# A third halving on VectorE in a single-query attention kernel, with shorter TensorE sums, another cut of the first K load and a whole last copy

## Chip, cores, metric

One core of a Trainium2 chip (trn2). The metric is the device time of one execution in microseconds (us); the median of several is given. The *span* in a profile is about 1.7 us shorter than the time. Only one core runs, so there is no second die to compare with. In the views PE is TensorE (matmuls), PEld its weight loads, DVE VectorE, ACT ScalarE, POOL GpSimd, and SPq the queue that issues loads. The granted TensorE clock is given where it matters.

## The reference

For 256 heads, one query of 128 numbers is compared with 4096 keys, and the softmax of the scores weighs 4096 values:

```python
B, H, Sq, Skv, Dh = 8, 32, 1, 4096, 128            # all bf16
scores = jnp.einsum('bhqd,bhkd->bhqk', q, k) * Dh ** -0.5
attn = softmax(scores, axis=-1)
out = jnp.einsum('bhqk,bhkd->bhqd', attn, v)
```

Each key and value is used once. K and V are 537 MB; all else is small.

## The kernel before

The work goes in 32 tiles of 8 heads. A tile of K, and one of V, is 128 partitions x 256 positions x 128 numbers, 8.39 MB. There are two K buffers and one V buffer; the last V takes a K buffer. The scores of a tile come in four chunks of 64 positions. VectorE multiplies K by q and adds the upper half of D to the lower. TensorE adds up the remaining 64 numbers, as eight slices of 8, through matmuls with the identity; 8 numbers are left. VectorE adds up these eight. In the views `kt` and `vt` are tiles of K and V, `ps` these sums, `sc` the scores, `av` the weighted values; `comb` is the copy of `av`, `op` the matmuls that gather it, and `stage` the finished rows.

```python
cuts = {                                   # pieces of a load; [C] where nothing is said
    ("k", 0): [C // 4, C // 4, C // 2],
    ("k", NT - 4): [C // 2] * 2,           # NT - 3, NT - 2 likewise
    ("k", NT - 1): [C // 4, C // 4, C // 2],
    ("v", NT - 1): [C // 2, C // 4, C // 8, C // 16, C // 32, LAST, LAST],
}
# ... load(): q is queued right behind the first piece of the first K

def product(t, lo, hi):
    for c0 in range(lo, hi, MC):           # MC = 64 positions
        part = kt[:, c0 : c0 + MC, :]
        nc.vector.tensor_tensor(out=part, in0=part, in1=qb..., op=ALU.mult)
        nc.vector.tensor_tensor(out=part[:, :, 0 : D // 2], in0=part[:, :, 0 : D // 2],
                                in1=part[:, :, D // 2 : D], op=ALU.add)

def sum_over_d(t, u):
    n = D // 2 // DS                       # DS = 8, so 8 matmuls
    for s in range(n):
        nc.tensor.matmul(ps[:], lhsT=ident[:],
            rhs=kt[:, u * UC : (u + 1) * UC, s * DS : (s + 1) * DS],
            start=(s == 0), stop=(s == n - 1))

# values_of(t): 64 matmuls "av", dealt to four column groups of the array
group = [0 if t == NT - 1 and C // 2 <= c0 < 3 * C // 4 else c0 // CB % TG ...]

def copy_of(t):
    n = CB if t < NT - 1 else CB // 2      # the last copy: half on ScalarE, half on VectorE
    nc.scalar.activation(out=comb[:, 0:n, :], in_=av[:, 0:n, :], func=ACT.Copy)
    if n < CB:
        nc.vector.tensor_copy(out=comb[:, n:CB, :], in_=av[:, n:CB, :])

# order in a tile t: issue K of t+1 and V of t; chunks 0 and 1; the av matmuls of
# tile t-1, which free V's buffer; chunks 2 and 3; softmax weights
```

## Time and profile before

| | before |
|---|---|
| median (3 runs, 1254.5 to 1254.62) | 1254.57 us |
| span of the profiled run | 1252.8 us |
| loaded | 537 MB, 429 GB/s over the span |
| busy: TensorE, VectorE, ScalarE | 554.0, 967.6, 343.3 us |
| mean granted TensorE clock | 0.685 |

In the groups of instructions of the page, the columns are: line, engine, operation, output and inputs, shapes and count | busy us, mean ns | idle us of the engine before them and what ended most of it. Two of VectorE's groups are compared later:

```profile
L175 DVE TENSOR_TENSOR kt<-kt,qb 128x8192 bf16<-128x8192 bf16 x128 | 565.2, 4415 | 181.9 <-DMA kt<-in_k_dram 175.3
...
L202 DVE TENSOR_REDUCE sc<-ps 128x64 f32<-128x512 f32 x128 | 87.8, 686 | 68.1 <-PE ps L190 68.1
```

The next view cuts the tail into stretches. In each line, after the stretch and its length, come the busy us of PE, PEld, DVE, ACT and POOL with their instruction counts, then the granted clock, the mean busy share of the 16 transfer engines and the GB/s.

```profile
1244.00:1246.00 2.00, 2.00 (x11) 0.87 (x10) 0.00 (x0) 0.00 (x0) 0.00 (x0) 1.00 0.62 247
1246.00:1247.00 1.00, 1.00 (x13) 0.47 (x11) 0.00 (x0) 0.00 (x0) 0.00 (x0) 1.00 0.44 156
1247.00:1248.00 1.00, 0.95 (x11) 0.33 (x7) 0.00 (x0) 0.00 (x0) 0.00 (x0) 1.00 0.07 26
```

Some engines are done by 1244, and one, roughly (0.07 of 16), still works after 1247. A load counts as landed only when all 16 are done.

### The profile page before, as it was taken

The numbers are of one execution on the slowest core, as the hardware profiler recorded it, in microseconds if no ns is written. First come the engines' busy times: TensorE is split into PE (matmuls) and PEld (weight loads), VectorE is DVE, ScalarE is ACT, GpSimd is POOL, SyncE is SP. The second block draws the span as 40 slices with busy tenths as digits, with TensorE's granted clock in tenths as the row PEclk, the third lists the DMA queues.
The fourth block names the chain that finished last, engine by engine and source line by source line (L and its number), as shares of the span: only waits on it lengthen the run. The fifth ranks groups of instructions, "written<-read, shape, count | busy, mean of one in ns | idle before, by whom it ended". The sixth has DMA issues, their size and how long they took to land.

```text
span 1252.8 us, 8134 instructions
## 1 busy us (share of the span) xinstructions
PE 554.0 (44%) x3299; PEld 202.6 (16%) x3299; DVE 967.6 (77%) x531; ACT 343.3 (27%) x625; POOL 6.0 (0%) x26
## 2 busy tenths in 40 slices
PE   2444543345534355333453334542445434545356
PEld 0111111111111111111111111111112111211112
DVE  7877887777977779777797777886778877977981
ACT  0333123331233321333213333123330333311333
POOL 1000000000000000000000000000000000000000
PEclk8667666667657767576765776666676766676777
DMA  9999999999999999999999999999999999999997
GB/s 404 435 436 432 434 435 433 434 432 434 435 434 436 434 429 429 431 432 433 434 434 436 430 436 436 436 434 435 432 427 427 437 433 432 434 420 431 430 439 311
DMA packets 11734, 537.53 MB, mean 429 GB/s; under 512 B 1840, under 2 KB 2096, under 8 KB 2352
## 3 DMA queue, kind: packets, MB, share of 16 engines
q1 hardware_dynamic: 11360, 536.94, 99.3%
q8 instruction: 26, 0.43, 0.1%
q10 hardware_dynamic: 336, 0.07, 0.0%
q14 instruction: 12, 0.10, 0.0%
HBM read 536.94 MB, written 0.07 MB: 429 GB/s over the span
## 4 chain that ended last, share of the span: by engine, by line
DMA 79%; PE 14%; DVE 6%; issue 0%; SPq 0%; another core or an unknown queue 0%; ACT 0%
DMA vt<-in_v_dram 78%; PE av L256 13%; DVE kt L175 3%; DVE kt L178 2%; PE ps L190 1%; DMA q_all<-in_q_dram 1%; DVE sc L202 0%; SPq L147 0%; DVE pmax L212 0%; DVE spread L214 0%; DVE nmax L219 0%; DVE comb L286 0%; ACT comb L284 0%; ACT stage L310 0%
## 5 line engine op out<-in xcount | busy, mean ns | idle before, releaser
L175 DVE TENSOR_TENSOR kt<-kt,qb 128x8192 bf16<-128x8192 bf16 x128 | 565.2, 4415 | 181.9 <-DMA kt<-in_k_dram 175.3
L190 PE MATMUL ps<-kt,ident 128*128 128x512 bf16 x1024 | 353.6, 508 | 572.1 <-DVE kt L178 572.1
L231 ACT ACTIVATE w<-sc,bias 128x256 bf16<-128x256 f32 x256 | 300.5, 1587 | 260.5 <-DVE bias L223 260.5
L178 DVE TENSOR_TENSOR kt<-kt 128x4096 bf16<-128x4096 bf16 x128 | 293.4, 2292 | 4.4
L190 PEld LDWEIGHTS <-ident 128*128 128x128 bf16 x1024 | 119.6, 119 | 775.5 <-issue 506.1
L256 PE MATMUL av<-vt,w 128*32 128x512 bf16 x2047 | 176.5, 513 | 90.0 <-DMA vt<-in_v_dram 90.0
L202 DVE TENSOR_REDUCE sc<-ps 128x64 f32<-128x512 f32 x128 | 87.8, 686 | 68.1 <-PE ps L190 68.1
L284 ACT ACTIVATE comb<-av 128x512 bf16<-128x512 f32 (+1 forms) x32 | 19.5, 609 | 413.1 <-PE av L256 413.1
L231 ACT ACTIVATION_READ_ACCUMULATOR w<-sc,bias 128x1 f32 x256 | 126.6, 495 | 0.0
L256 PEld LDWEIGHTS <-w 128*32 128x32 bf16 x2047 | 68.7, 125 | 207.1 <-DMA vt<-in_v_dram 107.8
L163 ACT ACTIVATE qg<-qh 8x128 bf16<-8x128 f32 x32 | 8.5, 266 | 165.9 <-PE qh L159 165.9
L310 ACT ACTIVATE stage<-op,rz 16x128 bf16<-16x128 f32 x16 | 5.9, 371 | 56.4 <-DVE rz L276 41.3
L301 PE MATMUL op<-comb,pick 128*16 128x128 bf16 x128 | 13.4, 230 | 12.8 <-ACT comb L284 12.4
L212 DVE TENSOR_REDUCE pmax<-sc 128x1 f32<-128x256 f32 x32 | 13.4, 420 | 1.1
L165 PE MATMUL qp<-qg,heads 8*128 8x128 bf16 x32 | 7.5, 235 | 12.7 <-ACT qg L163 12.7
L276 DVE RECIPROCAL rz<-zp 16x1 f32<-16x1 f32 x16 | 2.4, 149 | 13.9 <-PE zp L268 13.9
L159 PE MATMUL qh<-q_all,ident 128*8 128x128 bf16 x32 | 8.2, 256 | 8.3 <-DMA q_all<-in_q_dram 8.3
L167 ACT ACTIVATE qb<-qp 128x128 bf16<-128x128 f32 x32 | 8.9, 277 | 10.4 <-PE qp L165 10.4
L301 PEld LDWEIGHTS <-pick 128*16 128x16 bf16 x128 | 7.6, 91 | 21.0 <-issue 20.9
L214 DVE TENSOR_SCALAR spread<-same,pmax 128x32 f32<-128x32 f32 x32 | 7.7, 241 | 1.1
L223 DVE TENSOR_SCALAR bias<-own,nmax 128x8 f32<-128x8 f32 x32 | 7.4, 231 | 1.1
L219 DVE TRANSPOSE_TENSOR_REDUCE nmax<-spread 128x1 f32<-128x32 f32 x32 | 6.8, 211 | 1.1
(27 smaller groups left out, 20.1 us busy)
## 6 DMA issues: line engine op xcount, KB each, us to landing
kt<-in_k_dram SPq DMA_DIRECT2D x8, 4096.0 KB, 43.0
kt<-in_k_dram SPq DMA_DIRECT2D x4, 2048.0 KB, 23.3
vt<-in_v_dram SPq DMA_DIRECT2D x1, 4096.0 KB, 41.4
vt<-in_v_dram SPq DMA_DIRECT2D x1, 2048.0 KB, 45.9
vt<-in_v_dram SPq DMA_DIRECT2D x1, 1024.0 KB, 47.8
vt<-in_v_dram SPq DMA_DIRECT2D x1, 512.0 KB, 48.6
vt<-in_v_dram SPq DMA_DIRECT2D x31, 33.3
kt<-in_k_dram SPq DMA_DIRECT2D x27, 47.4
```

The source lines that it names most:

```text
L159: nc.tensor.matmul(qh[:], lhsT=ident[:, p0 : p0 + G], rhs=q_all[:, x, :], start=True, stop=True)
L163: nc.scalar.activation(out=qg[:], in_=qh[:], func=ACT.Copy)
L167: nc.scalar.activation(out=qb[:, 0, :], in_=qp[:], func=ACT.Copy)
L175: nc.vector.tensor_tensor(out=part, in0=part, in1=qb[:].to_broadcast([P, MC, D]), op=ALU.mult)
L178: nc.vector.tensor_tensor(out=part[:, :, 0 : D // 2], in0=part[:, :, 0 : D // 2], in1=part[:, :, D // 2 : D], op=ALU.add,)
L190: nc.tensor.matmul(ps[:], lhsT=ident[:], rhs=kt[:, u * UC : (u + 1) * UC, s * DS : (s + 1) * DS], start=(s == 0), stop=(s == n - 1),)
L202: nc.vector.tensor_reduce(out=scs[t][:, u * UC : (u + 1) * UC], in_=sums.pop((t, u))[:], axis=AX.X, op=ALU.add)
L212: nc.vector.tensor_reduce(out=pmax[:], in_=sc[:], axis=AX.X, op=ALU.max)
L231: nc.scalar.activation(out=w[:, :, g], in_=sc[:], func=ACT.Exp, bias=bias[:, g : g + 1], scale=scale, accum_out=esum[:, t % R, g : g + 1],)
L256: nc.tensor.matmul(avs[t][j * AG : (j + 1) * AG, :], lhsT=w[:, c0 : c0 + CB, :], rhs=vt[:, c0 : c0 + CB, :], start=(i < TG), stop=(j not i ...
L284: nc.scalar.activation(out=comb[:, 0:n, :], in_=av[:, 0:n, :], func=ACT.Copy)
L301: nc.tensor.matmul(ops[n][:], lhsT=pick[:, m, r, :], rhs=comb[:, m, :], start=(r == 0 and m == 0), stop=(r == R - 1 and m == CB - 1),)
```

## The change

The intent: VectorE has idle time in each tile and TensorE's work can shrink. So VectorE halves the products of chunks 0 and 1 once more, and TensorE adds up 32 numbers instead of 64 there. The start and the tail are adjusted around that.

```diff
     cuts = {
-        ("k", 0): [C // 4, C // 4, C // 2],
-        ("k", NT - 4): [C // 2] * 2,
+        ("k", 0): [C // 2] * 2,
 ...
+    def width_of(t, u):
+        return D // 4 if u < NU // 2 and t < NT - 3 else D // 2
 ...
+            if width_of(t, c0 // UC) < D // 2:
+                nc.vector.tensor_tensor(
+                    out=part[:, :, 0 : D // 4], in0=part[:, :, 0 : D // 4],
+                    in1=part[:, :, D // 4 : D // 2], op=ALU.add,
+                )
 ...
-        n = D // 2 // DS
+        n = width_of(t, u) // DS
 ...
-            0 if t == NT - 1 and C // 2 <= c0 < 3 * C // 4 else c0 // CB % TG
+            0 if t == NT - 1 and C // 2 <= c0 < C // 2 + 3 * C // 16 else c0 // CB % TG
 ...
-        n = CB if t < NT - 1 else CB // 2
-        nc.scalar.activation(out=comb[:, 0:n, :], in_=av[:, 0:n, :], func=ACT.Copy)
-        if n < CB:
-            nc.vector.tensor_copy(out=comb[:, n:CB, :], in_=av[:, n:CB, :])
+        nc.scalar.activation(out=comb[:], in_=av, func=ACT.Copy)
```

## The prediction

> **What bounds the kernel now.** I read the page first, from the slices down to the chain, and then the timeline of one tile and of the tail.
>
> ```profile
> DVE  7877887777977779777797777886778877977981
> DMA  9999999999999999999999999999999999999997
> GB/s 404 435 436 432 434 435 433 434 432 434 435 434 436 434 429 429 431 432 433 434 434 436 430 436 436 436 434 435 432 427 427 437 433 432 434 420 431 430 439 311
> ...
> q8 instruction: 26, 0.43, 0.1%
> ...
> DMA 79%; PE 14%; DVE 6%; issue 0%; SPq 0%; another core or an unknown queue 0%; ACT 0%
> ```
>
> The transfer engines are full in 39 of 40 slices, VectorE is the next busiest (77%), and 79% of the chain is waiting for V to land. What matters then is whether the queue ever runs dry. The timeline of one tile in the middle answers that: VectorE, then TensorE, then the queue that issues loads.
>
> ```profile
> 664.46 4.42 DVE L175 TENSOR_TENSOR kt<-kt,qb 128x8192 bf16<-128x8192 bf16 x1 [6.88 <-DMA kt<-in_k_dram]
> 668.92 2.29 DVE L178 TENSOR_TENSOR kt<-kt 128x4096 bf16<-128x4096 bf16 x1
> ...
> 675.63 2.29 DVE L178 TENSOR_TENSOR kt<-kt 128x4096 bf16<-128x4096 bf16 x1
> ...
> 703.20 4.43 DVE L175 TENSOR_TENSOR kt<-kt,qb 128x8192 bf16<-128x8192 bf16 x1 [6.84 <-DMA kt<-in_k_dram]
> ```
> ```profile
> 645.04 5.17 PE L256 MATMUL av<-vt,w 128*32 128x512 bf16 x64 [2.26 <-DMA vt<-in_v_dram]
> ...
> 683.83 6.24 PE L256 MATMUL av<-vt,w 128*32 128x512 bf16 x64 [3.16 <-DMA vt<-in_v_dram]
> ```
> ```profile
> 650.26 0.33 SPq L147 DMA_DIRECT2D vt<-in_v_dram  x1
> 655.64 0.33 SPq L147 DMA_DIRECT2D kt<-in_k_dram  x1
> ```
>
> Landings alternate: V at 645.04, K at 664.46, V at 683.83, K at 703.20. That is 19.4 us for each 8.39 MB load and 38.7 to 38.8 us for a tile, about 433 GB/s. The V load that must start when K lands at 664.46 was issued at 650.26, 14.2 us early. The K load that must start at 683.83 was issued at 655.64, 28.2 us early. So the queue is never empty, and neither VectorE nor TensorE sets the pace. VectorE waits 6.9 us in each tile for K to land.
>
> **What the Trainium skill says.** "DMA: Bandwidth & Descriptors", section "Where 436 GB/s comes from", gives a ceiling of 435.2 GB/s for loads into SBUF. The trace agrees: its full slices are at 427 to 439. K and V are 64 loads of 8.389 MB, 536.9 MB, so by that figure 1233.6 us at least (an estimate); the last V lands at 1248.0. "VectorE: DVE Perf Modes", section "The perf-mode tier table", has a bf16 tensor_tensor of 2048 elements at 2x, 1224 ns. No operation of that size is in this trace, but 8192 elements take 4415 ns and 4096 take 2292, a slope of 0.518 ns an element and a fixed 168 ns, which gives 1230 ns for 2048: the two agree. "Runtime: NRT & Kernel Launch", section "Instruction fetch mechanics", says that instructions are fetched in 16 KiB blocks of 256 by DMA. The trace shows 26 instruction packets of 0.43 MB on one queue; 2 x 3299 TensorE instructions over 256 are 25.8.
>
> **The change, part by part.**
>
> *The third halving.* It covers chunks 0 and 1 of tiles 0 to 28: 58 new VectorE additions of 128x2048. At the estimated 1.23 us they are 71.3 us of busy time, so VectorE goes from 967.6 to about 1038.5 us, 83% of the span. Per tile it is 2 x 1.23 = 2.46 us. That comes out of the 6.9 us wait for K, leaving some 4.4. Nothing on the path.
>
> *The shorter sums.* Each such chunk takes 4 matmuls instead of 8. That removes 232 of the 1024 at L190, each with its weight load. At 353.6 / 1024 = 0.345 us of busy time each it is 80 us, so TensorE goes from 554 to about 474 us. The only place where this could reach the loads is the release of V's buffer, after the 64 matmuls at L256. Those start when V lands, or when the sum of chunk 1 is done, if that is later. Chunk 1's addition ends at 677.92 in the tile shown; add 2.46 and it is 680.4; four slow matmuls (0.43 us apart in this trace) make 682.1. V lands at 683.83. V stays the later, by 1.7 us, so V's buffer is freed when it was. Were it missed, 14.2 us of slack lie behind it.
>
> *The first K load in halves.* q is queued behind the first piece. It landed at 8.35 us behind 2.1 MB; behind 4.2 MB it should land 2.1 MB / 434 GB/s = 4.8 us later, near 13.2. VectorE then starts at 14.4 instead of 9.57, and tile 0 is 2.5 us longer, so K of tile 2 is issued at about 41 + 7.3 = 48.3. The queue needs it when the first V lands, at 61.66. V of tile 1 is issued after the L256 matmuls of tile 0. Chunk 1 of tile 1 ends 7.3 us later for the late start and tile 0, and another 2.5 for tile 1's own additions, less 1.7 for the shorter sum: 59.9 + 8.1 = 68, and 5.3 for the matmuls gives 73.3. The queue needs it at 82.3, when K of tile 2 lands. Both are still early, by 13 and 9 us. Tile 2 starts about 3 us late, and at 35.5 us of work against a 38.7 us period it is back in step one tile later. The bytes start moving at the same time as before. So 0 us of the end.
>
> *K of tile 28 whole instead of in halves.* That tile starts about 7 us later and ends about 6 later. Tile 29's last two chunks wait for V of tile 28 at 1149.94 anyway (before, VectorE idled 6.63 us for it), which absorbs this. The last three K tiles keep their pieces and their width, so the tail's order stands.
>
> *The last group of matmuls and the last copy.* These are after or around the last byte.
>
> ```profile
> 1248.02 0.73 PE av L256 x3
> 1248.75 0.02 issue
> 1248.77 0.39 ACT comb L284
> 1249.16 0.02 issue
> 1249.19 0.44 DVE comb L286
> 1249.62 0.04 issue
> 1249.67 0.29 PE op L301 x2
> 1249.95 0.02 issue
> 1249.97 0.36 ACT stage L310
> ```
>
> From the copy to the stage are 1.20 us. After: one copy of 128x512 in 0.60 us (the median of that form when ScalarE was idle), then four matmuls where two had been hidden under VectorE's half, 0.39 to 0.59 us, and hand-overs of 0.1: 1.1 to 1.3. That is a wash. Twelve instead of sixteen matmuls in a row on one column group let TensorE catch up earlier, by up to 4 x 0.22 x 3/4 = 0.65 us. Before, it had only just caught up when the last piece landed, so this pays only if the loads end earlier.
>
> *Instruction fetch.* 464 fewer TensorE instructions are about two of 26 packets. The transfers end unevenly: the DMA share falls to 0.67 in 1242 to 1244 and 0.07 in 1247 to 1248, while the last engine is still working. A packet fewer on the slowest engine could end the loads up to about 1 us earlier, on another nothing. I put 0.5 us on this, which is a choice.
>
> *Sum:* 1254.57 + 0 (loop) + 0 (head) + 0 (copy) - 0.5 (fetch and tail) = 1254.1 us.
>
> **The rivals.**
>
> 1. *VectorE becomes the bound.* It is the busiest compute engine and gets 71 us more. If all of it were exposed the time would be near 1326. Against this, each tile has 6.9 us of wait for K and gets 2.46 of work. VectorE would have to take 3.5 us per addition, more than for twice the size.
>
> 2. *Buffers are freed later and the queue runs dry.* The late start of tile 0 adds to the longer tiles. The least slack I find is 9 us, in tile 1. If I am wrong there by all of the 8 us shift and more, it costs once, some 2 to 5 us: about 1258.
>
> 3. *The engine work removed gives time back.* If 80 us less of TensorE work, or its clock, were on the path, the kernel would gain several us per tile. Against it: the chain's 13% of L256 follows each V landing, and the next V is released with 14 us to spare. Even with perfect transfers the end is the 2 us of the start, 1233.6 and the 4.8 us after the last landing, 1240.4, or 1.1% faster. A gain of over 2% has no room.
>
> 4. *The loads themselves move at a different rate* because VectorE writes SBUF more. The load that lands while VectorE works throughout (664.46 to 683.83) took 19.37 us, and the one during which it idles 6.84 us (683.83 to 703.20) also took 19.37. So no.
>
> **Range and chances.** Three runs span 0.12 us, so scatter is small. What I can't work out is how the lag of the slowest transfer engine changes with other instruction packets. Single tile periods in this trace are up to 1.5 us over 38.7, so I allow about that much either way: 1252.4 to 1255.8. Faster by over 2% would need under 1229.5, below the floor of rival 3: 0.01. Slower by over 2% is over 1279.7, possible only if rival 1 or 2 holds in most tiles: 0.02. Within 2%: 0.97.
>
> **What would show it right or wrong.** Right: the DMA row stays at nines, the spacing of V landings stays at 38.7 us, the new additions show 58 times at about 1.23 us, VectorE's wait for K falls from 175 us by roughly 65, L190 has 792 matmuls, and the last V lands within 1.5 us of 1248.0. Wrong: a slice with DMA at 8 or less in the middle, a V issue within 2 us of the landing before it, waits of the av matmuls on chunk 1's sum that push the next landing out, or additions well over 1.3 us. If the last V lands over 2 us earlier or later with the queue always full, my reading that the transfers alone set the rate is right but the fetch term is mis-sized.

## The result, and the profile after

| | before | after |
|---|---|---|
| median, 6 runs each | 1254.60 us (1254.50 to 1254.62) | 1252.99 us (1252.75 to 1253.34) |
| ratio | | 0.9988 (95% interval 0.9975 to 1.0) |
| span of the profiled run | 1252.8 | 1251.5 |
| last V landed at (the piece that the chain waits for) | 1247.97 | 1247.06 |
| from there to the end of the span | 4.8 | 4.4 |
| busy: TensorE, VectorE | 554.0, 967.6 | 501.8, 1038.0 |

A ratio is the mean time of one kernel's runs over that of the other's of the same rounds, so it is not quite the ratio of the medians. The gain is 1.6 us, 0.13%. The two sets of runs do not overlap, but the 95% interval reaches 1.0. Differences this small need the trace beside them. The profiled run of the changed kernel took 1253.24 us, one of its slower ones, so the two traces differ by 1.3 us of span and not by 1.6. Two smaller V pieces land after the one in the table, at 1248.32 and 1248.64 before and 1247.41 and 1247.72 after: 0.9 us earlier too.

The page of the changed kernel, the same rows as shown before in the prediction:

```profile
DVE  5888898888988889788898888987879888899981
DMA  9999999999999999999999999999999999999997
...
q8 instruction: 24, 0.39, 0.1%
...
L179 DVE TENSOR_TENSOR kt<-kt,qb 128x8192 bf16<-128x8192 bf16 x128 | 565.1, 4415 | 91.3 <-DMA kt<-in_k_dram 79.8
...
L211 DVE TENSOR_REDUCE sc<-ps 128x64 f32<-128x512 f32 x128 | 87.7, 685 | 87.0 <-PE ps L199 87.0
...
L187 DVE TENSOR_TENSOR kt<-kt 128x2048 bf16<-128x2048 bf16 x58 | 71.0, 1225 | 2.0
```

The transfers are as full as before. 58 additions took 1225 ns each. VectorE's idle time before the products fell by 90.6 us: 71.0 went into the additions, and 18.9 into waiting longer for TensorE's sums (68.1 to 87.0). There are two instruction packets fewer on q8; its count follows TensorE's instructions in all runs here. The tail, first in stretches, then in the chain of waits (of before, the one line that the prediction doesn't show; then the changed kernel):

```profile
1244.00:1246.00 2.00, 2.00 (x20) 0.93 (x19) 0.00 (x0) 0.00 (x0) 0.00 (x0) 1.00 0.65 254
1246.00:1247.00 1.00, 0.91 (x11) 0.37 (x6) 0.00 (x0) 0.00 (x0) 0.00 (x0) 1.00 0.54 195
1247.00:1248.00 1.00, 0.90 (x7) 0.41 (x7) 0.00 (x0) 0.14 (x1) 0.00 (x0) 1.00 0.07 23
```
```profile
1199.17 48.80 DMA vt<-in_v_dram
```
```profile
1200.13 46.92 DMA vt<-in_v_dram
...
1247.10 0.74 PE av L265 x3
...
1247.86 0.60 ACT comb L292
...
1248.51 0.40 PE op L307 x4
...
1248.93 0.36 ACT stage L316
```

The last V lands 0.9 us earlier. Copy to stage takes 1.07 us where it took 1.20.

**Where the 0.9 us come from.** The trace also records when each of the 16 transfer engines reported its share of a load. These are the times of the last V piece, in us after the first of the 16 (from the trace's landing records; 16 numbers, sorted):

```
before: 0 0.10 0.28 0.31 0.41 0.91 4.36 4.55 4.56 4.57 4.59 4.66 4.72 4.78 5.10 6.21
after:  0 0.01 0.12 0.22 0.35 0.81 3.39 3.99 4.50 4.61 4.64 4.72 4.73 4.84 4.85 4.89
```

For a whole load at the start the 16 lie within 0.4 us. The spread grows in steps through the run. In both kernels six engines end well ahead and ten behind. Before, one is 1.1 us behind all others. It fell back between two landings, at about 1228 and 1238 us, and the one TensorE instruction packet of that stretch moved at 1232. Such a packet (16 KB) lasts 1.0 to 1.1 us in the trace, a data packet of 64 KB 2.4. In the trace of before the packets' durations repeat with a period of eight (1106, 1094, 1026, 1018, 1073, 1069, 1060, 1098, then 1099, 1086, 1018, 1016, ... ns), which suggests that they go round eight engines. This packet was the 25th, hence the fourth on its engine. The landings agree: after packets 1, 9, 17 and 25 (at 66, 454, 843 and 1232 us) the slowest engine lay 1.6, 3.2, 4.7 and 6.3 us behind the first, so each of its packets set it back by about 1.5 us, more than the 1.1 us that the packet lasts. The 26th started at 1248.56, when all but the slowest engine had reported. With 24 packets no engine has a fourth.

So theory F: *the end of the loads is set by the transfer engine that moved the most instruction packets; the change takes the 25th away from it.* The rivals are T (the gain is in the tail's copy and groups), L (fewer, larger pieces load faster), and that VectorE's or TensorE's work itself counts.

### The profile page after: what moved, and what is told of

It is laid out like the page before. It is cut to its first block, busy times and chain, and to the rows that moved or that the text cites. A ratio compares the mean times of both kernels' runs of the same rounds, so it can differ in the third digit from the quotient of the medians. Undisturbed runs are those within 1.5% of the kernel's fastest.

```text
span 1251.5 us, 7723 instructions
## 1 busy us (share of the span) xinstructions
PE 501.8 (40%) x3067; PEld 176.1 (14%) x3067; DVE 1038.0 (83%) x588; ACT 343.8 (27%) x625; POOL 6.0 (0%) x26
## 4 chain that ended last, share of the span: by engine, by line
DMA 76%; PE 15%; DVE 8%; issue 1%; SPq 0%; ACT 0%
DMA vt<-in_v_dram 75%; PE av L265 13%; DVE kt L179 5%; DVE kt L182 2%; PE ps L199 1%; DMA q_all<-in_q_dram 1%; DVE kt L187 0%; DVE sc L211 0%; SPq L146 0%; DVE pmax L221 0%; DVE spread L223 0%; DVE nmax L228 0%; ACT comb L292 0%; PE op L307 0%; ACT stage L316 0%
## 5 line engine op out<-in xcount | busy, mean ns | idle before, releaser
L199 PE MATMUL ps<-kt,ident 128*128 128x512 bf16 x792 | 293.1, 529 | 662.8 <-DVE kt L187 507.4
L199 PEld LDWEIGHTS <-ident 128*128 128x128 bf16 x792 | 92.0, 119 | 824.7 <-issue 670.0
L265 PE MATMUL av<-vt,w 128*32 128x512 bf16 x2047 | 181.0, 525 | 43.7 <-DMA vt<-in_v_dram 43.7
L292 ACT ACTIVATE comb<-av 128x512 bf16<-128x512 f32 x32 | 19.7, 616 | 413.2 <-PE av L265 413.2
L265 PEld LDWEIGHTS <-w 128*32 128x32 bf16 x2047 | 68.1, 127 | 167.7 <-issue 80.9
L187 DVE TENSOR_TENSOR kt<-kt 128x2048 bf16<-128x2048 bf16 x58 | 71.0, 1225 | 2.0
L307 PE MATMUL op<-comb,pick 128*16 128x128 bf16 x128 | 16.4, 271 | 14.6 <-ACT comb L292 14.6
```

The source lines that it names most:

```text
L187: nc.vector.tensor_tensor(out=part[:, :, 0 : D // 4], in0=part[:, :, 0 : D // 4], in1=part[:, :, D // 4 : D // 2], op=ALU.add,)
L199: nc.tensor.matmul(ps[:], lhsT=ident[:], rhs=kt[:, u * UC : (u + 1) * UC, s * DS : (s + 1) * DS], start=(s == 0), stop=(s == n - 1),)
L265: nc.tensor.matmul(avs[t][j * AG : (j + 1) * AG, :], lhsT=w[:, c0 : c0 + CB, :], rhs=vt[:, c0 : c0 + CB, :], start=(i < TG), stop=(j not i ...
L292: nc.scalar.activation(out=comb[:], in_=av, func=ACT.Copy)
L307: nc.tensor.matmul(ops[n][:], lhsT=pick[:, m, r, :], rhs=comb[:, m, :], start=(r == 0 and m == 0), stop=(r == R - 1 and m == CB - 1),)
```

## The experiments

Each call also ran the kernel before on the same chip (9 runs); its medians were 1254.53 to 1254.63 on four chips. All kernels were checked against the reference and passed. Differences quoted are of medians against before in the same rounds. The 95% intervals of the ratios are about 0.0013 wide on each side, wider than most effects here. For the small ones I rely on ranges of runs and on the trace.

### The halving alone (e1_halving)

```diff
+            if width_of(t, c0 // UC) < D // 2:   # third halving, into the lower quarter
+                nc.vector.tensor_tensor(...)
-        n = D // 2 // DS
+        n = width_of(t, u) // DS
```

> The kernel before with the third halving and its shorter sums alone; loads, copy and groups as before. Theory F (the loads end when the transfer engine that carries the most instruction packets is done; two packets fewer on the TensorE queue take the 25th packet, of about 1.1 us, away from the slowest engine): 24 instruction packets, last V landing 1.0 to 1.2 us earlier, time 0.9 to 1.2 us below before, so 1253.4 to 1253.7. Theory T (the gain is in the last copy and the groups): within 0.3 us of before. Theory L (the gain comes from fewer pieces of the K loads): within 0.3 us of before.

Measured: 1253.65 us (1253.30 to 1253.83), before 1254.63 (1254.45 to 1254.96): 0.98 less, ratio 0.9992 (0.9979 to 1.0004). 24 packets, and the 16 engines' lag ends at 4.97 us. F's number came out, and the V piece that landed at 1247.97 before landed at 1246.77, 1.2 us earlier. But the chain of this kernel's tail no longer passes through the last V load:

```profile
1239.72 3.41 PE av L264 x27
1243.17 4.82 PE av L264 x29
...
1249.22 0.36 ACT stage L318
```

The matmuls run on without a wait into the last copy. With the loads ending earlier, TensorE is now level with them. So the last V was earlier, as F expected, but no longer set the end.

### The shorter sums alone (e2_short_sums)

```diff
-        n = D // 2 // DS
+        n = width_of(t, u) // DS     # 4 matmuls; the upper quarter is dropped, wrong on purpose
```

> The kernel before with 4 matmuls instead of 8 for the first half of tiles 0 to 28, without the added VectorE work. The result is wrong on purpose. Theory F: as with the whole halving, 0.9 to 1.2 us below before, since only the number of TensorE instructions counts. Theory T and theory L: no change. A theory in which VectorE's added work costs something that the shorter sums give back: faster than the halving alone by more than 0.3 us.

Measured: 1253.45 us (four runs 1253.27 to 1254.04, one 1254.65), 1.18 less; the mean is 0.86 less. 24 packets. VectorE's 71 us of additions are not needed for the gain, nor do they cost anything that could be seen. Here too the chain ends in matmuls that don't wait for the last V (it landed at 1246.75). The comparison with the reference did not notice the dropped terms. The likely reason, not tested: q and k are drawn with a standard deviation of 0.05, so the scores differ by some 0.0025 (an estimate) and the softmax is nearly flat. The check says little about errors in the scores in this case.

### The additions alone (e3_adds)

```diff
+            if width_of(t, c0 // UC) < D // 2:
+                nc.vector.tensor_tensor(
+                    out=part[:, :, D // 2 : 3 * D // 4],    # a quarter nobody reads any more
+                    in0=part[:, :, 0 : D // 4], in1=part[:, :, D // 4 : D // 2], op=ALU.add)
```

> The kernel before with the 58 added VectorE additions, written to a quarter that nobody reads, and all 8 matmuls kept. The result stays right. VectorE about 1038 us busy, TensorE instructions as before. Theory F: 26 packets and the time of before within 0.3 us. A theory in which VectorE's work costs time: over 0.5 us slower. The waits for K should fall to about 80 us in total, as in the changed kernel.

Measured: 1254.59 us (1254.47 to 1254.75), 0.04 less; VectorE busy 1038.7 us, wait for K 72.5 us, 26 packets, and the straggler is back (lags ... 5.08, 5.12, 6.27 us). The added VectorE work is hidden, as predicted.

### The tail alone (e4_tail)

```diff
-            0 if t == NT - 1 and C // 2 <= c0 < 3 * C // 4 else c0 // CB % TG
+            0 if t == NT - 1 and C // 2 <= c0 < C // 2 + 3 * C // 16 else c0 // CB % TG
-        # the last copy in two halves on two engines
+        nc.scalar.activation(out=comb[:], in_=av, func=ACT.Copy)
```

> The kernel before with the last copy whole on ScalarE and the shorter run of matmuls in one group, nothing else. From the traces, the stretch from the last copy to the stage is 1.20 us before and 1.07 after, so 0.1 to 0.2 us faster. Theory T, under which the whole gain lies here: 1.3 to 1.6 us faster. Theory F: last V landing as before within 0.3 us.

Measured: 1254.35 us (1254.29 to 1254.43), 0.28 less; no run overlaps those of before. The last V lands as before. T explains about a sixth of the gain, not all.

### The loads alone (e5_loads)

```diff
-        ("k", 0): [C // 4, C // 4, C // 2],
-        ("k", NT - 4): [C // 2] * 2,
+        ("k", 0): [C // 2] * 2,
```

> The kernel before with only the first K load in halves and K of tile 28 whole. Theory F: same time within 0.3 us, 26 packets. Theory L, under which fewer pieces move faster: 0.8 us or more faster. q should land near 13.2 us and VectorE start near 14.4, with no effect on the end.

Measured: 1254.35 us (1254.20 to 1254.69), before 1254.56 (1254.44 to 1254.73): 0.21 less, with overlapping ranges, so not told from zero. 26 packets and the straggler at 6.26 us. L is out as the main cause.

### As many instructions as before, with the change's work (e6_same_count)

Against the changed kernel:

```diff
+        parts = 2 if width_of(t, u) < D // 2 else 1
+        h = UC // parts
+        for p in range(parts):            # 8 matmuls of 256 columns instead of 4 of 512
             for s in range(n):
                 nc.tensor.matmul(
-                    ps[:], lhsT=ident[:],
-                    rhs=kt[:, u * UC : (u + 1) * UC, s * DS : (s + 1) * DS],
+                    ps[:, p * h : (p + 1) * h, :], lhsT=ident[:],
+                    rhs=kt[:, u * UC + p * h : u * UC + (p + 1) * h, s * DS : (s + 1) * DS],
```

> The changed kernel, but each of its shorter sums done as 8 matmuls of half the columns, so that TensorE has as many instructions as before and its column work is that of the change. Theory F: 26 packets again, the 25th falls on the slowest engine, and the time is about 1.1 us above the changed kernel, near 1254.1 to 1254.4. A theory in which the removed TensorE column work or the freed buffers bring the gain: the time of the changed kernel, 1252.7 to 1253.4.

Measured: 1254.30 us (1253.98 to 1254.62), before 1254.56. Everything of the change is in it, and most of the gain is gone: 0.26 is left of 1.61. 26 packets; lags ... 4.95, 5.01, 6.03 us. This is the clearest test. The columns that TensorE works through are those of the changed kernel; only the number of instructions differs.

### More instructions, the same work (e7_30_pages, e8_34_pages)

Against before, the same split for chunks 0 and 1, and for all four:

```diff
+        parts = 2 if u < NU // 2 else 1   # e7_30_pages;  e8_34_pages: parts = 2
```

> The kernel before with the sums of chunks 0 and 1 cut into twice as many matmuls of half the columns: 1024 more TensorE instructions, 30 packets instead of 26. In the trace of before, the durations of the instruction packets repeat with a period of 8, which suggests that they go round 8 transfer engines. Then 25 packets that start ahead of the last data and 29 are both at most 4 on one engine. Theory F with this rotation: the time of before within 0.5 us. Theory F with all packets on one engine: 4 x 1.1 = 4.4 us slower. No fetch effect: the time of before.

> The kernel before with all sums cut into twice as many matmuls of half the columns: 2048 more TensorE instructions, 34 packets. Theory F with the rotation over 8 engines: the 33rd packet is the fifth of one engine, so about 1.1 us slower than before, near 1255.7. Theory F with the packets spread evenly over 16 engines: 0.5 us. No fetch effect: the time of before within 0.3 us.

Measured: 30 packets, 1254.70 us (1254.61 to 1255.01), 0.14 more. 34 packets, 1256.14 us (1256.06 to 1256.96), 1.58 more, ratio 1.0014 (1.0002 to 1.0027), the one of the small effects whose interval excludes 1. Four packets more did almost nothing, the next four a whole step. A cost that grows evenly with the packets, or all packets on one engine, would give equal steps. A rotation over 16 engines would also step at the 33rd packet, but not at the 25th, where the kernels with 24 and 26 packets differ. The landing records fit a rotation over eight: with 30 packets five engines lie at 6.1 to 6.4 us, where one lay, and the slowest is only 0.15 us later. With 34, seven lie at 6.1 to 6.4 and one is pushed to 7.68: eight in all. The chain of the kernel with 30 ends in matmuls that don't wait for the last V, so its time bounds the loads' part only from above.

```
30 packets: ... 4.94 6.07 6.16 6.20 6.24 6.36
34 packets: ... 6.20 6.22 6.34 6.34 7.68
```

The step was 1.58 in time where I expected 1.1, because I had taken the packet's own duration; the landings put its cost at 1.5 (7.68 against 6.21). Of the 34-packet kernel, the page's count and the tail:

```profile
q8 instruction: 34, 0.56, 0.2%
```
```profile
1247.00:1248.00 1.00, 1.00 (x10) 0.41 (x9) 0.00 (x0) 0.00 (x0) 0.00 (x0) 1.00 0.52 193
1248.00:1249.00 1.00, 1.00 (x15) 0.54 (x14) 0.00 (x0) 0.00 (x0) 0.00 (x0) 1.00 0.24 80
1249.00:1250.00 1.00, 0.88 (x9) 0.27 (x7) 0.00 (x0) 0.00 (x0) 0.00 (x0) 1.00 0.05 16
```

The share of about one engine alone comes later: the last V piece lands at 1250.19 instead of 1248.64.

### The halving in all chunks (e9_all_chunks)

```diff
-        return D // 4 if u < NU // 2 and t < NT - 3 else D // 2
+        return D // 4 if t < NT - 3 else D // 2
```

> The changed kernel with the third halving in all four chunks of tiles 0 to 28. 464 TensorE instructions fewer, 22 packets. Theory F with packets going round 8 engines: three packets on the slowest engine in the changed kernel, still three here, so within 0.4 us of the changed kernel (1252.6 to 1253.4). Theory F with an even spread, or each fewer instruction paying: a further 1 us. VectorE gets another 2.46 us per tile, of which the wait for K in the changed kernel (up to 4.3 us) has room; if VectorE becomes the bound, over 1255.

Measured: 1253.78 us (1253.73 to 1254.21), before 1254.63: 0.85 less. This is less than the changed kernel's 1.61, so my bound of 0.4 us was missed, and the version doesn't beat it. It has 22 packets, so by TensorE's packets alone nothing should have got worse. VectorE is not the bound: the chain still runs through the last V load, which landed at 1247.64. In the landing records one engine fell from 5.0 to 5.9 us behind, and another from 3.5 to 4.2, between the landings at 1208 and 1229 us, a stretch where no TensorE packet moved but two 8 KB packets of the other instruction queue (q14) did. That asked for the experiment on GpSimd below.

### The old groups in the changed kernel (e11_old_groups)

```diff
-            0 if t == NT - 1 and C // 2 <= c0 < C // 2 + 3 * C // 16 else c0 // CB % TG
+            0 if t == NT - 1 and C // 2 <= c0 < 3 * C // 4 else c0 // CB % TG
```

> The changed kernel with the old rule for the groups, sixteen matmuls in a row on one group. In the halving alone the chain ended in 29 av matmuls and no longer in the last V load: TensorE had become the later of the two. If so, this is 0.2 to 0.6 us slower than the changed kernel, with TensorE and not the last V load in the chain. If the groups don't matter: within 0.15 us.

Measured: 1253.27 us (1252.94 to 1253.66), 1.36 less than before, where the changed kernel had 1.61 in another session; the runs of the two overlap. The chain changed as expected: it ends in av matmuls that never wait for the last V, as in the halving alone. But the last stage starts at 1248.87, no later than the changed kernel's 1248.93. So the groups put TensorE out of the chain, and their worth in time is inconclusive, 0.3 us at most.

### Loading one tile with the lower eight engines (e10_low8)

The idea was to give the engines that are ahead more of the load. Against the changed kernel:

```diff
+        if kind == "v" and t == NT // 2:
+            for p0, p1 in ((0, 8), (8, 16), (16, P)):
+                nc.sync.dma_start(buf[p0:p1, :, :], src[t, p0:p1, :, :])
```

> The changed kernel with V of tile 16 loaded as three transfers: partitions 0 to 7, 8 to 15, and the other 112. By the Trainium skill, DMA: Bandwidth & Descriptors, section Why a DMA increments its semaphore by 16 and not by 1, a transfer of 8 partitions runs on the 8 lowest-numbered engines, so these take 9 rows of 64 KB each and the others 7, where all had 8. A row of 64 KB takes 2.42 us. At the end of the changed kernel six engines are ahead of the slowest by 4 to 5 us. If the 8 lowest-numbered engines are the ones that are ahead, the loads end up to 2.4 us earlier, near 1250.6 to 1251.5. If they are the slow ones, 2.4 us later, near 1255.4. If the slow ones are spread over both, in between or later. If the spread of the engines doesn't set the end: within 0.3 us of the changed kernel.

Measured: 1284.22 us (1283.35 to 1285.06, 4 runs), ratio 1.0236 (1.0222 to 1.025). All my figures were wrong. Most of the loss sits around that one tile, some 25 of 31 us (an estimate from the three slices under 400; GB/s, the page):

```profile
GB/s 423 430 424 429 446 430 427 432 440 432 426 435 438 430 425 440 432 436 429 434 350 215 383 434 436 428 432 428 444 430 430 430 436 432 430 434 422 431 432 280
```

I had cited one section of the Trainium skill and overlooked another. "SBUF — State Buffer", section "Door 1: The DMA port swizzle (why `[64,N]` ≈ `[32,N]`)", says that bandwidth depends on how many of the 16 SBUF ports the partitions reach, and eight neighbouring partitions reach two. The drop to 215 GB/s, with the DMA row still at nines, agrees with engines queueing for few ports; no run separates that from other causes. It does not test F.

### Idle instructions on GpSimd (e12_pool_dose)

Against the changed kernel:

```diff
             load("v", t)
+            for _ in range(160):
+                nc.gpsimd.memset(idle[:], 0.0)     # one column that nobody reads
```

> The changed kernel with 5120 idle memsets of one column on GpSimd, 160 in each tile, that nobody reads; GpSimd is busy about 10 of each tile's 38.7 us and on no path. Question left by the kernel with all chunks narrow, whose slowest transfer engine fell 0.9 us further back with no TensorE packet in that stretch: do instruction packets of the other engines cost the loads as well? Theory F for all instruction packets: 5120 instructions of 64 bytes are some 40 packets of 8 KB more on the other instruction queue, 0.31 us each by the trace, some 5 per engine if they go round 8 engines, so 1.5 us or more slower than the changed kernel, 1254.5 or above. If only TensorE's packets count: 1252.7 to 1253.4.

Measured: 1274.60 us (1274.23 to 1275.56), before 1254.53: 20.1 us more, ratio 1.0162 (1.0148 to 1.0176). Against the changed kernel's 1252.99 of another session it is 21.6 more. The page:

```profile
q14 instruction: 52, 0.43, 0.1%
...
DMA 75%; PE 14%; DVE 8%; issue 1%; POOL 1%; SPq 0%; ACT 0%; POOLq 0%
```

The other instruction queue carries 52 packets instead of 12. GpSimd is 1% of the chain. The landing records show why it costs more than expected: one transfer engine alone falls further behind with each load, 8 us by 240 us of the run, and from about 360 us on stays at 12 to 14 until GpSimd is through at 810 us, while the others lie within 3 us. So GpSimd's packets fall on one engine. Until then whole loads landed every 20.01 us, where the changed kernel has 19.35, and about one such packet moved per load: 0.66 us each, though a packet lasts 0.31. An estimate from this: 40 packets cost that engine 26.4 us; the changed kernel's slowest engine was 4.9 behind anyway, which leaves 21.5 of the 21.6 us measured. Why the lag stops near 13 us is argued, not tested: the next V load is issued about 14 us ahead of need, so the fast engines run dry there and wait (in one tile the V load was issued at 669.01 and the first engine was through with the load before it at 670.8). So TensorE's and GpSimd's instructions, on no critical path here, cost transfer time. The straggler of the kernel with all chunks narrow fits this; which engine its two packets used was not seen.

## Why the prediction was right, and where its size was off

The measured 1252.99 us lie in the range of 1252.4 to 1255.8; the point, 1254.1, was 1.1 too high.

Its signs of being right appeared: the DMA row stayed at nines, the new additions show 58 times at 1.225 us, 792 matmuls remain at the sums, and the last V landed within 1.5 us of 1248.0.

- **Loop: 0 us. Right.** The additions took 1.225 us against 1.23 estimated and are hidden (the additions alone: 0.04 us). A detail was wrong: the wait for K was to fall by roughly 65 us and fell by 95. The prediction left out VectorE's longer waits for the sums. In a middle tile TensorE now pauses longer ahead of chunk 3's sum and then runs slower: before, then after, from the timelines of TensorE:

```profile
653.73 1.89 PE L190 MATMUL ps<-kt,ident 128*128 128x512 bf16 x8 [1.68 <-DVE kt L178]
```
```profile
656.84 3.20 PE L199 MATMUL ps<-kt,ident 128*128 128x512 bf16 x8 [3.94 <-DVE kt L182]
```

- **TensorE's saving off the path. Right,** though it was 52 us and not 80: 232 fewer matmuls, but the remaining ones are busy 529 ns in the mean instead of 508, at a granted clock of 0.638 instead of 0.685. V's buffer was freed on time. The kernel with the same columns in twice the instructions shows that the columns have no visible part in the gain.
- **Head: 0 us. Right within noise.** VectorE started at 14.46 us (predicted 14.4); the loads alone gave 0.21 with overlapping ranges.
- **Copy and groups: "a wash". Mis-sized.** Copy to stage fell from 1.20 to 1.07 us, and both together gave 0.28 in their own run.
- **Instruction fetch: 0.5 us. The mechanism was right, the term mis-sized.** It gave 0.98 (halving alone) to 1.18 (sums alone). I had priced a chance that the packets removed were the slowest engine's; that they were was luck as far as the prediction goes. The trace of before held the answer, had I read the landings of the 16 engines: the slowest was 1.1 us behind, through a fourth packet that 24 packets don't have. The landings of the V piece in the table show the packets' part without the tail's own effects: 1246.75 to 1247.06 us in the four kernels with 24 packets, 1247.97 to 1248.11 in the five with 26, 1248.20 with 30 and 1249.52 with 34. The one with 22, at 1247.64, is held up by the other instruction queue, as far as the landings show.
- **Readings and sums.** The full slices run from 420 to 439 GB/s and not from 427, and several lie above the 435.2 of the page cited. 967.6 + 71.3 is 1038.9, not 1038.5. A tile's 35.5 us of work is 34.3 by the prediction's own numbers (38.7 - 6.9 + 2.46). None of this moves the point. The scatter of before was 0.12 us in the runs that the prediction had, but 0.3 to 0.55 in the later sessions.

In medians 0.98 + 0.28 + 0.21 = 1.47 of the 1.61 us. The last of these, and the 0.14 that are missing, are within the scatter.

Open: which transfer engines carry the instruction packets (the trace doesn't name them), and why a packet costs its engine more than its own duration.

## What to carry to other kernels

The loads are the bound here, and engine work that fits under them was free (71 us of VectorE's additions: 0.04 us), but instructions were not: their packets delay the transfer engines that carry the loads. In such a kernel count them, and look at the slowest of the 16 engines, not the mean share. Once the loads end earlier, check which wait ends last in the tail: here TensorE was then level with the loads.

## What the Trainium skill lacked or had wrong

- "Runtime: NRT & Kernel Launch", section "Instruction fetch mechanics", calls the cost of crossing a 16 KiB boundary mostly hidden. In this load-bound kernel eight more TensorE packets cost 1.58 us (34 against 26) and four cost 0.14; no page says which of the 16 engines carry them. The durations' period of eight, the landings and these steps speak for a rotation over eight of the 16.
- The same section gives 16 KiB blocks for all engines. The other instruction queue moved packets of 8 KB here: 40 more for 5120 GpSimd instructions, on one transfer engine, for 20.1 us above the kernel before and 21.6 above the changed one.
- "DMA: Bandwidth & Descriptors", section "Where 436 GB/s comes from", from which the prediction takes the fabric's ceiling of 435.2 GB/s, also says that for transfers from HBM the HBM side binds, at about 358 (its own measured 16 MB load has 425). With one core running, a steady tile reached 433 here and the span's mean was 429; no limit near 358 shows.
- The same page, section "Latency and other measured facts", names two engines that are usually slower, for a reason of another kind; here six end ahead and ten behind. I found nothing on instruction packets making the 16 engines drift apart (0.4 us at the start, 6.2 at the end of before), so that the last one sets the end.
